# Start of the load order, the place of an arc tangent, and the engines of a power table in a fused state-space and feed-forward kernel

## The chip, the cores and the metric

One core of one Trainium2 chip runs the kernel. The metric is the device time of one execution in microseconds (us). TensorE (PE, with its weight load PEld), VectorE (DVE), ScalarE (ACT), GpSimd (POOL) and SyncE (SP) work side by side; DMAs are started from the queues of SP, ScalarE and GpSimd. Lines are named L12 and so on by their place in the kernel before.

## The reference, cut to what matters

```python
xn = layernorm(x)                         # x: 2048 rows of 576
# A: a long convolution of each of the 576 channels, by its response K
dt = exp(log_dt)
K[d, l] = Re( sum_n C[d, n] * exp(dt * A[d, n] * l) * dt * B[d, n] )      # n < 128, l < 2048
yA = causal_convolution(K, xn) + xn * Dskip
# B: a feed-forward layer
yB = silu(xn @ w1) @ w2                   # w1: 576 x 4608, w2: 4608 x 576
out = x + yA + yB
```

## The kernel before, in words

Rows of x are taken as 16 tiles of 128 (j = 0 to 15), each gathered by four loads of 32 partitions (`quarters`, L73), two tiles to a load (`load_x`, L161). `norm` (L174) takes the statistics on VectorE (L181, L182), the power -0.5 on GpSimd (L186), and the normalisation itself on VectorE for even tiles (L190) and on ScalarE for odd ones (L195). `put_xt` (L118) turns a tile over by TensorE (L122, L126) and splits it into a rounded part and the rest, xh and xl, ScalarE taking the first (L123, L127) and VectorE the second (L124, L128). Every product of the feed-forward layer is made of three matmuls of such parts.

The feed-forward layer (`ffn`, L229) goes over two halves of the rows, and in each over 9 chunks of 512 columns of w1, in blocks of four row tiles. `up` (L290) makes one 128 x 512 piece of the hidden layer in a PSUM tile ph (a ring of two), of which ScalarE makes gf and gh (L306, L307) and VectorE gl (L308); `down` (L310) multiplies by w2 into po (L328), which VectorE adds to acc (L333). The first block's `up` is done in two halves of 256 columns: tiles 0 and 1 first, tiles 2 and 3 after. Weights are loaded raw (w1r and w2r, L237 to L288) and split in the same way (L266, L268, L284, L286). In the second half a part of the products goes by a scheme with fewer multiplications (`wino_ffn`).

The other layer is a side line, a generator (`side`, L1024) that `weave` (L31) advances as the feed-forward layer comes on. It makes the tables of the response from the parameters (`natural`, L639: an arc tangent at L726 and a reciprocal root at L728, behind the last gh that was issued), tiles 8 to 15 in between; then the response (`kgen`, L756) in 36 steps of 16 channels, between some 150 and 650 us. A step makes angles, sines and magnitudes; every second step `powers` (L790) makes the powers 0 to 7 of four bases (lags 256, 64, 8 and 1) by multiplications on VectorE (L798 to L800) in the table pw, where only the powers 0 to 3 of lag 64 are used. TensorE sums over n (kp, L864) and transforms (z, L879); ScalarE puts the result into `stage` (L887), and after every fourth step two stores put it into DRAM (d1k, L892), each of 64 partitions with 64 runs of 32 numbers. In the same stretch `spread` (L138) transforms xn and stores it from GpSimd (d1u, L157), out of one buffer u1 for each of 32 steps. Afterwards `spectral` and `tail` finish the convolution.

What sets the order: each engine and each DMA queue runs its instructions in order, and that order isn't the one of the text. A planner arranges the instructions by a simulated timeline, by the order of the text as priority; `tc.high_priority()` lets an instruction go ahead, and `behind(ins)` (L135) keeps the instructions in its block behind `ins` on the same engine. At the start the side line runs tiles 0 to 3 wholly, then `ffn` asks for its first weights (the pair for t = 0 on GpSimd's queue, the rest on SP's) and splits them, then tiles 4 to 7 follow (L1077 to L1082). The loads of tiles 0 to 3 alternate between SP's and ScalarE's queues, and the stores of the first eight normalised tiles (dxn, L227) are SP's. From the beginning of `kgen` on, a second buffer w1x lets the raw first-layer weights be asked for a group ahead (`next_w1`, L253).

## Time and profile before

| | us |
|---|---|
| median of 3 runs | 1114.02 (1113.07 to 1114.62) |
| the profiled execution | 1115.58 |
| its span, first to last instruction | 1113.8 |
| TensorE busy in the span | 1090.6 |
| VectorE busy | 950.6 |
| ScalarE busy | 725.8 |
| GpSimd busy | 140.5 |

The granted TensorE clock was 1.00. Busy times overlap, so they don't add up to the span. In rows of the timeline the first number is the start and the second the duration, in us, of so many instructions (x4) in a row; what stands in square brackets is the idle time of the engine ahead of them and what ended it. In rows of groups, behind the bar, stand the busy time in us and the mean of one in ns, then the idle time ahead of them. Rows of waits give the sum in us, the number and the longest. Rows of one line give the smallest, middle and largest duration in ns and the first and last start in us. Rows of DMA issues end with the median time from issue to landing in us.

### The profile page before, as it was taken

The page shows a single profiled execution, that of the slowest core. Times are in us where ns is not written, and L with a number is a line of the kernel's source. Part 1 is how long each engine was busy: PE and PEld are TensorE (multiplying, and loading weights), DVE is VectorE, ACT ScalarE, POOL GpSimd, SP SyncE. Part 2 cuts the span into 40 slices and gives each one's busy share as a digit, 9 for nine tenths or more (in the row PEclk, how much of TensorE's full clock was granted, in tenths as well). Part 3 has the DMA queues.
Part 4 walks back from the last instruction along what each step waited for, and adds up shares of the span by engine and source line. Part 5 has one row for each costly group of instructions (what it writes and reads, how often), then busy time and mean ns, then how long its engine had stood idle before and what let it go on. Part 6 is the DMA issues. An engine that isn't in the chain of part 4 may idle for free.

```text
span 1113.8 us, 23080 instructions
## 1 busy us (share of the span) xinstructions
PE 1090.6 (98%) x9101; PEld 987.0 (89%) x9101; DVE 950.6 (85%) x1615; ACT 725.8 (65%) x1285; POOL 140.5 (13%) x244
## 2 busy tenths in 40 slices
PE   6999999999999999999999999999999999999998
PEld 5987989889988898898999888899899999999787
DVE  6699899999999999998999978989888988886333
ACT  4675455776767766667667646878687888775320
POOL 1022100000000000000330001121111211111220
PEclk9999999999999999999999999999999999999999
DMA  9445632436353536356964235465456555553985
GB/s 274 141 161 180 190 124 84 143 84 172 111 148 125 153 117 173 113 124 243 257 177 91 92 84 173 133 183 165 145 175 186 180 161 167 169 161 106 222 219 133
DMA packets 161869, 173.68 MB, mean 156 GB/s; under 512 B 88496, under 2 KB 127424, under 8 KB 161120
## 3 DMA queue, kind: packets, MB, share of 16 engines
q1 hardware_dynamic: 137200, 106.75, 34.4%
q0 software_dynamic: 23888, 63.67, 19.0%
q10 hardware_dynamic: 672, 1.77, 0.7%
q8 instruction: 72, 1.18, 0.4%
q14 instruction: 37, 0.30, 0.1%
HBM read 109.64 MB, written 62.60 MB: 155 GB/s over the span
## 4 chain that ended last, share of the span: by engine, by line
PE 83%; DVE 7%; DMA 5%; ACT 2%; issue 1%; POOL 0%; SPq 0%; DVEq 0%; ACTq 0%; POOLq 0%
PE po L328 35%; PE ph L298 19%; PE pb L453 6%; PE pc L453 3%; PE kp L864 3%; PE pu L996 2%; PE pk L996 2%; PE pb L996 2%; PE pa L453 2%; PE ph L299 2%; PE ph L300 2%; DMA w<-dw 1%; PE z L879 1%; DMA w1r<-in_B_w_dram 1%; PE pc L459 1%
## 5 line engine op out<-in xcount | busy, mean ns | idle before, releaser
L328 PE MATMUL po<-w,gh 128*128 128x288 f32 x2304 | 476.3, 297 | 5.1 <-DMA w<-dw 1.8
L328 PEld LDWEIGHTS po<-w,gh 128*128 128x128 f32 x2304 | 375.7, 188 | 21.9 <-issue 4.0
L328 PE MATMUL po<-w,gl 128*128 128x288 f32 x1152 | 334.7, 295 | 0.6 <-DVE gl L308 0.6
L328 PEld LDWEIGHTS po<-w,gl 128*128 128x128 f32 x1152 | 215.0, 188 | 2.6 <-DVE gl L308 0.9
L333 DVE TENSOR_TENSOR acc<-po,acc 128x288 f32<-128x288 f32 x296 | 130.1, 451 | 63.7 <-PE po L328 62.4
L298 PE MATMUL ph<-xh,w1h 128*128 128x512 f32 (+1 forms) x368 | 99.0, 387 | 0.9 <-ACT xh L123 0.6
L298 PE MATMUL ph<-xl,w1h 128*128 128x512 f32 (+1 forms) x368 | 98.4, 385 | 0.0
L298 PE MATMUL ph<-xh,w1l 128*128 128x512 f32 (+1 forms) x368 | 97.8, 382 | 0.0
L306 ACT ACTIVATE gf<-ph 128x512 f32<-128x512 f32 (+1 forms) x92 | 53.2, 579 | 59.2 <-PE ph L300 42.9
L298 PEld LDWEIGHTS ph<-xl,w1h 128*128 128x128 f32 x368 | 67.6, 191 | 12.9
L298 PEld LDWEIGHTS ph<-xh,w1l 128*128 128x128 f32 x368 | 66.4, 188 | 11.7
L298 PEld LDWEIGHTS ph<-xh,w1h 128*128 128x128 f32 x368 | 65.1, 191 | 11.2 <-ACT xh L123 0.9
L157 POOL DMA_DIRECT2D d1u<-u x32 | 17.5, 547 | 405.9 <-ACT u L156 404.6
L823 ACT ACTIVATE c<-th,magic 128x1040 f32<-128x1040 f32 x36 | 42.0, 1166 | 40.3 <-DVE C L844 28.3
L307 ACT CAST gh<-gf 128x512 fp32r<-128x512 f32 (+1 forms) x92 | 55.3, 602 | 14.6 <-PE po L328 13.7
L308 DVE TENSOR_TENSOR gl<-gf,gh 128x512 fp32r<-128x512 f32 (+1 forms) x92 | 60.7, 661 | 3.5 <-ACT gh L307 3.3
L901 POOL DMA_DIRECT2D m<-in_cm_dram x64 | 33.9, 531 | 234.0 <-PE pu L996 118.0
L825 ACT ACTIVATE c<-th 128x1040 f32<-128x1040 f32 x36 | 38.7, 1075 | 33.8 <-DVE th L824 33.6
L470 DVE TENSOR_TENSOR gl<-gf,gh 128x512 fp32r<-128x512 f32 x56 | 37.8, 688 | 19.1 <-ACT gh L469 18.5
L843 DVE TENSOR_TENSOR S<-th,C 128x1024 f32<-128x1024 f32 x36 | 43.9, 1221 | 11.7 <-ACT th L826 11.6
L824 DVE SCALAR_TENSOR_TENSOR th<-c,th 128x1040 f32<-128x1040 f32 x36 | 44.4, 1235 | 0.7 <-ACT c L823 0.6
L807 DVE TENSOR_TENSOR th<-vt,fT 128x1040 f32<-128x1040 f32 x36 | 44.4, 1235 | 0.0
(271 smaller groups left out, 2373.0 us busy)
## 6 DMA issues: line engine op xcount, KB each, us to landing
w1r<-in_B_w_dram SPq DMA_DIRECT2D x35, 512.0 KB, 4.2
dw<-w SPq DMA_DIRECT2D x28, 576.0 KB, 4.4
w<-dw POOLq DMA_DIRECT2D x28, 576.0 KB, 5.7
w2r<-in_B_w_dram SPq DMA_DIRECT2D x44, 288.0 KB, 5.0
d1u<-u POOLq DMA_DIRECT2D x32, 288.0 KB, 2.7
d1k<-stage SPq DMA_DIRECT2D x18, 512.0 KB, 7.2
ul<-d1u SPq DMA_DIRECT2D x32, 288.0 KB, 2.9
kl<-d1k SPq DMA_DIRECT2D x32, 288.0 KB, 3.4
```

The source lines that it names most:

```text
L298: nc.tensor.matmul(ph, w[:, kt, :], v[:, kt, a:e], start=n + kt == 0, stop=False)
L306: nc.scalar.activation(gf, ph, AF.Silu)
L307: pins["gh"] = nc.scalar.copy(gh, gf).ins
L308: pins["gl"] = nc.vector.tensor_sub(gl, gf, gh).ins
L328: pins["pe"] = nc.tensor.matmul(po[:, :HD], gs[g][:, js], ws[:, w, hs], start=n == 0 and j not in begun, stop=n == 3 * len(terms) - 1, ski ...
L333: nc.vector.tensor_add(acc[j][:, hs], po[:, :HD], acc[j][:, hs])
L453: pins["pe"] = nc.tensor.matmul(dst, a[:, kt], v[:, kt], start=start and n == 0, stop=stop and n == 5, skip_group_check=True).ins
L807: nc.vector.tensor_mul(split(th), row(vt[:, 0:65], 65), col(fT, i, 65))
L823: nc.scalar.activation(c65, th, AF.Identity, bias=magic)
L824: nc.vector.scalar_tensor_tensor(th, c65, MAGIC, th, op0=ALU.subtract, op1=ALU.subtract)
L843: nc.vector.tensor_mul(ov3, t[:, :, 0:64].rearrange("n d (x y) -> n d x y", y=32), mv3)
L996: nc.tensor.matmul(dst, st, mv[:, hs], start=n == 0, stop=n == 3 * len(terms) - 1)
```

## The change

Seven things change. Tiles 0 and 1 are loaded by eight loads of one tile instead of four of two, normalised one after the other, both on VectorE, and only then turned over, tile 0's xl behind tile 1's normalisation. The start goes in turns: loads of tiles 0 and 1; all six loads of the first w1 pieces, now all on SP's queue; tiles 0 and 1, then the loads of tiles 2 and 3, on SP's queue alone; loads of w2 and the w1 splits, the first of which is behind tile 0 on ScalarE and the others behind tile 1; tiles 2 and 3, behind tile 1; the w2 splits; tiles 4 to 7. The stores of normalised tiles 0 to 7 go to GpSimd's queue. The arc tangent is issued behind the latest odd tile's normalisation on ScalarE too. In the power table, ScalarE's Square makes powers 2 and 4, lag 64 comes last, and its powers 4 to 7 aren't made. The stores of the response go from SP's to GpSimd's queue. The buffer w1x is used from the third step of `kgen` on.

```diff
--- before.py
+++ after.py
@@ -115,13 +115,14 @@
         x4 = xtp.tile([P, 512], F32R, tag="x4", name=f"x4_{blk}")
         return xh, xl, x4
 
-    def put_xt(xh, xl, x4, src):
+    def put_xt(xh, xl, x4, src, low=None):
 
         pt = pss.tile([P, NKT, P], F32, tag="pss", name="pt")
         for kt in range(NKT):
             nc.tensor.transpose(pt[:, kt, :], src[:, kt * P:(kt + 1) * P], ident)
         nc.scalar.copy(xh, pt)
-        nc.vector.tensor_sub(xl, pt, xh)
+        with behind(low):
+            nc.vector.tensor_sub(xl, pt, xh)
         pt = pss.tile([P, 512], F32, tag="pss", name="pt4")
         nc.tensor.transpose(pt[:64, :P], src[:, NKT * P:D], ident)
         pins["xt_s"] = nc.scalar.copy(x4[:64, :], pt[:64, :P]).ins
@@ -161,8 +162,12 @@
     def load_x(j, pool, tag, engines):
 
         t = pool.tile([P, 2, D], F32, tag=tag, name=f"{tag}{j}")
-        for ps, v, eng in quarters(xv, engines):
-            eng.dma_start(t[ps], v[:, j:j + 2])
+        for i in range(j, j + 2, 1 if j == 0 else 2):
+            for ps, v, eng in quarters(xv, engines):
+                if j == 0:
+                    eng.dma_start(t[ps, i], v[:, i])
+                else:
+                    eng.dma_start(t[ps], v[:, j:j + 2])
         pairs[j] = t
         return t[:, 0, :], t[:, 1, :]
 
@@ -186,31 +191,35 @@
         pins["sd"] = nc.gpsimd.tensor_tensor(sd[:, :n], sd[:, :n], mhalf[:, :n], op=ALU.pow).ins
         xn = p0.tile([P, 2, D], F32, tag="xn", name="xn") if js[0] < 8 else pairs[js[0]]
         for i, j in enumerate(js):
-            if j % 2 == 0:
+            if j % 2 == 0 or n == 1:
                 pins["xn"] = nc.vector.tensor_scalar(xn[:, i, :], xs[i], mv[:, i, 0:1], sd[:, i:i + 1],
                                                  op0=ALU.subtract, op1=ALU.mult).ins
             else:
                 nc.vector.scalar_tensor_tensor(mb[:, i:i + 1], mv[:, i, 0:1], -1.0, sd[:, i:i + 1],
                                                op0=ALU.mult, op1=ALU.mult)
-                nc.scalar.activation(xn[:, i, :], xs[i], AF.Identity,
-                                     scale=sd[:, i:i + 1], bias=mb[:, i:i + 1])
+                pins["xo"] = nc.scalar.activation(xn[:, i, :], xs[i], AF.Identity,
+                                                  scale=sd[:, i:i + 1], bias=mb[:, i:i + 1]).ins
         return xn
 
     def phase0(p0, js):
         j0 = js[0]
         if j0 < 8:
-            xs = load_x(j0, accp, "acc", (nc.sync, nc.scalar) if j0 < 4 else (nc.sync,))
+            xs = load_x(j0, accp, "acc", (nc.sync, nc.scalar) if j0 == 0 else (nc.sync,))
             acc.update(zip(js, xs))
+            yield
         else:
             xs = load_x(j0, p0, "xj", (nc.sync,))
         if j0:
-            normed(p0, js, xs)
+            with behind(pins["xt1"] if j0 == 2 else None):
+                turned(p0, js, norm(p0, js, xs))
         else:
-            for j, xj in zip(js, xs):
-                normed(p0, (j,), (xj,))
-
-    def normed(p0, js, xs):
-        xn = norm(p0, js, xs)
+            xn = [norm(p0, (j,), (xj,)) for j, xj in zip(js, xs)]
+            last = pins["xn"]
+            for j in js:
+                turned(p0, (j,), xn[j], None if j else last)
+                pins[f"xt{j}s"] = pins["xt_s"]
+
+    def turned(p0, js, xn, low=None):
         for i, j in enumerate(js):
             b, jj = divmod(j, 4)
             if b < 2:
@@ -218,13 +227,12 @@
                     xts[b] = new_xt(b)
                 c = slice(jj * P, (jj + 1) * P)
                 xh, xl, x4 = xts[b]
-                put_xt(xh[:, :, c], xl[:, :, c], x4[:, c], xn[:, i, :])
+                put_xt(xh[:, :, c], xl[:, :, c], x4[:, c], xn[:, i, :], low)
             else:
                 xt = p0.tile([P, 9, P], F32R, tag="xt", name="xt", bufs=1)
                 put_xt(xt[:, 0:4, :], xt[:, 4:8, :], xt[:, 8, :], xn[:, i, :])
                 nc.gpsimd.dma_start(dxt[b - 2][:, :, jj * P:(jj + 1) * P], xt.bitcast(F32))
-        eng = nc.sync if js[0] < 8 else nc.gpsimd
-        eng.dma_start(dxn[:, js[0]:js[0] + len(js)], xn[:, :len(js)])
+        nc.gpsimd.dma_start(dxn[:, js[0]:js[0] + len(js)], xn[:, :len(js)])
 
     def ffn():
         w2v = w2.rearrange("(t p) d -> p t d", p=P)
@@ -240,7 +248,7 @@
             first = half == 0 and c == 0
             r1 = (pa if first and t else w1x if t and w1x else wp).tile([P, 5, 2 * P], F32, tag="w1r", name="w1r", bufs=1)
             fs = slice(f * P, (f + 2) * P)
-            eng = nc.gpsimd if first and t == 0 else nc.sync
+            eng = nc.sync
             eng.dma_start(r1[:, 0:4, :], w1[0:512, fs].rearrange("(k p) f -> p k f", p=P))
             eng.dma_start(r1[0:64, 4, :], w1[512:576, fs])
             pins["load"] = eng.dma_start(r1[64:128, 4, :], w1[512:576, fs]).ins
@@ -262,7 +270,7 @@
                 h1 = wp.tile([P, 5, P], F32R, tag="w1h", name="w1h", bufs=FT + 1)
                 l1 = wp.tile([P, 5, P], F32R, tag="w1l", name="w1l", bufs=FT + 1)
                 src = r1[:, :, i * P:(i + 1) * P]
-                with behind(pins.get("gh", pins["xt1s"] if t else None)):
+                with behind(pins.get("gh", pins["xt1s" if t + i else "xt0s"])):
                     nc.scalar.copy(h1, src)
                 with behind(pins["xt1"] if first else None):
                     pins["w1l"] = nc.vector.tensor_sub(l1, src, h1).ins
@@ -345,10 +353,12 @@
 
         for t in (0, 2):
             load_w1(0, 0, t)
+        yield 0
+        for t in range(FT):
+            load_w2(0, 0, t)
         for t in (0, 2):
             split_w1(0, 0, t)
-        for t in range(FT):
-            load_w2(0, 0, t)
+        yield 0
         for t in range(FT):
             split_w2(0, 0, t)
         yield 0
@@ -685,7 +695,7 @@
 
         ex = nat.tile([P, 4 * D], F32, tag="ex", name="ex")
         r = nat.tile([P, 4 * D], F32, tag="r", name="r")
-        for k, lag in enumerate((256.0, 64.0, 8.0, 1.0)):
+        for k, lag in enumerate((256.0, 8.0, 1.0, 64.0)):
             nc.scalar.activation(ex.rearrange("n (d k) -> n k d", k=4)[:, k, :], lrT, AF.Tanh, scale=0.5 * lag)
         yield
 
@@ -722,7 +732,7 @@
         v.tensor_scalar(t1, t1, 1.0, None, op0=ALU.add)
         yield
 
-        with behind(pins["gh"]):
+        with behind(pins["gh"]), behind(pins["xo"]):
             last = nc.scalar.activation(t0, t0, AF.Arctan).ins
         with behind(last):
             last = nc.scalar.activation(bi, t1, AF.Abs_reciprocal_sqrt).ins
@@ -793,13 +803,14 @@
                 nc.scalar.copy(pw[:, :, :, :, 1].rearrange("n q (g c) k -> n q g (c k)", g=2),
                                bases.pop(0).rearrange("n g (q c) k -> n q g (c k)", q=2))
                 load_bases(i + 2)
-                pv = pw.rearrange("n r d k e -> n (r d k) e")
-                R = 2 * W * 4
-                nc.vector.tensor_mul(pv[:, :, 2], pv[:, :, 1], pv[:, :, 1])
-                nc.vector.tensor_mul(pv[:, :, 3:5], pv[:, :, 1:3], pv[:, :, 2:3].broadcast_to([P, R, 2]))
-                nc.vector.tensor_mul(pv[:, :, 5:8], pv[:, :, 1:4], pv[:, :, 4:5].broadcast_to([P, R, 3]))
+                pv = pw.rearrange("n r d k e -> n (r d) k e")
+                nc.scalar.activation(pv[:, :, :, 2], pv[:, :, :, 1], AF.Square)
+                nc.scalar.activation(pv[:, :, 0:3, 4], pv[:, :, 0:3, 2], AF.Square)
+                nc.vector.tensor_mul(pv[:, :, :, 3], pv[:, :, :, 1], pv[:, :, :, 2])
+                nc.vector.tensor_mul(pv[:, :, 0:3, 5:8], pv[:, :, 0:3, 1:4],
+                                     pv[:, :, 0:3, 4:5].broadcast_to([P, 2 * W, 3, 3]))
                 for q in range(2):
-                    nc.vector.tensor_mul(split(al[:, q]), split(pw[:, q, :, 1, 0:4]), col(rhoT, i + q, 4))
+                    nc.vector.tensor_mul(split(al[:, q]), split(pw[:, q, :, 3, 0:4]), col(rhoT, i + q, 4))
                 return al
 
             def head(i):
@@ -831,8 +842,8 @@
                     ak.unsqueeze(2).broadcast_to([P, W, 8, 4]))
                 nc.vector.tensor_mul(
                     mag[:, :, 32:96].rearrange("n d (x y) -> n d x y", y=8),
-                    pk[:, :, 2, :].unsqueeze(3).broadcast_to([P, W, 8, 8]),
-                    pk[:, :, 3, :].unsqueeze(2).broadcast_to([P, W, 8, 8]))
+                    pk[:, :, 1, :].unsqueeze(3).broadcast_to([P, W, 8, 8]),
+                    pk[:, :, 2, :].unsqueeze(2).broadcast_to([P, W, 8, 8]))
                 if i + 1 < NCK:
                     nxt = head(i + 1)
                     if i % 2 == 1:
@@ -889,7 +900,7 @@
                     d0 = (i // NRUN) * NRUN * CH
                     kv = d1k.rearrange("(k n) (g d) -> g n k d", n=64, g=2)
                     for gp_ in range(2):
-                        nc.sync.dma_start(kv[gp_, :, :, d0:d0 + NRUN * CH], stage[gp_ * 64:(gp_ + 1) * 64])
+                        nc.gpsimd.dma_start(kv[gp_, :, :, d0:d0 + NRUN * CH], stage[gp_ * 64:(gp_ + 1) * 64])
                 yield (i + 1) / NCK
 
         nc.gpsimd.dma_start(d1k.rearrange("(k n) d -> n k d", n=P)[0],
@@ -1028,7 +1039,9 @@
         with tc.tile_pool(name="pa", bufs=4) as pa:
             for js in ((0, 1), (2, 3), (4, 5), (6, 7)):
                 with behind(pins["xt3"] if js[0] > 2 else None):
-                    phase0(pa, js)
+                    for _ in phase0(pa, js):
+                        if js[0] <= 2:
+                            yield 0
                 pins[f"xt{js[1]}"], pins[f"xt{js[1]}s"] = pins["xt_v"], pins["xt_s"]
                 if js[0] == 2:
                     yield 0
@@ -1046,14 +1059,16 @@
                     else:
                         j = next(tiles)
                         with behind(pins["gl"]):
-                            phase0(pb, (j, j + 1))
+                            for _ in phase0(pb, (j, j + 1)):
+                                pass
             with behind(pins["sd"]):
                 nc.gpsimd.dma_start(f1, cf1)
             nc.sync.dma_start(vt, cv)
-            with tc.tile_pool(name="up", bufs=1) as up, tc.tile_pool(name="w1x", bufs=1) as w1x:
+            with tc.tile_pool(name="up", bufs=1) as up, tc.tile_pool(name="w1x", bufs=1) as more:
                 sp = spread(up)
                 for n, at in enumerate(kgen()):
                     if n > 1:
+                        w1x = more
                         next(sp, None)
                     yield marks[0] + at * (marks[1] - marks[0])
                 for _ in sp:
@@ -1074,11 +1089,9 @@
         yp = ctx.enter_context(tc.tile_pool(name="yp", bufs=3))
         yield from tail()
 
-    sd = side()
-    next(sd)
-    fg = ffn()
-    next(fg)
-    next(sd)
+    sd, fg = side(), ffn()
+    for g in (sd, fg, sd, fg, sd, fg, sd):
+        next(g)
     weave(fg, 276, sd)
     for j in range(8, 14, 2):
         store(pairs[j], j, (nc.sync, nc.scalar))
```

## The prediction

> **What bounds the kernel now.** First the page's head, then the busy times by stretch.
>
> ```profile
> span 1113.8 us, 23080 instructions
> PE 1090.6 (98%) x9101; PEld 987.0 (89%) x9101; DVE 950.6 (85%) x1615; ACT 725.8 (65%) x1285; POOL 140.5 (13%) x244
> ```
>
> ```profile
> core 0: us, PE busy (x) PEld busy (x) DVE busy (x) ACT busy (x) POOL busy (x), PEclk, DMA share, GB/s
> 0.00:30.00 30.00, 19.38 (x128) 18.16 (x129) 21.07 (x61) 15.00 (x31) 6.22 (x13) 1.00 0.96 266
> 60.00:150.00 90.00, 86.99 (x531) 78.02 (x530) 82.69 (x149) 52.00 (x79) 15.18 (x17) 1.00 0.60 192
> 150.00:650.00 500.00, 498.89 (x5139) 449.94 (x5140) 476.93 (x704) 338.73 (x504) 37.34 (x72) 1.00 0.48 137
> ```
>
> TensorE has 1113.8 - 1090.6 = 23.2 us without work, and no instruction of the change takes a matmul away, so only idle time can be won: 10.6 us before 30, 3.0 us between 60 and 150, 1.1 us in the 500 us in which the response is made (150 to 650). The rest lies in parts that the change doesn't touch. So the Squares and the stores, both in the long stretch, can win at most 1.1 us however much VectorE they save (it is busy 476.93 of 500 there, yet TensorE hardly waits for it). What counts is the start and the stretch from 60 to 150.
>
> The start, in order of time:
>
> ```profile
> 0.74 1.78 SPq L165 DMA_DIRECT2D acc<-in_A_u_dram  x4
> ...
> 5.62 1.54 DVE L181 BATCH_NORM_STATS2 st<-acc 128x6 f32<-128x288 f32 x4 [4.69 <-DMA acc<-in_A_u_dram]
> 7.54 1.22 POOL L186 TENSOR_TENSOR sd<-sd,mhalf 128x1 f32<-128x1 f32 x2 [3.72 <-DVE sd L185]
> 8.15 0.58 DVE L190 TENSOR_SCALAR xn<-acc,mv,sd 128x576 f32<-128x576 f32 x1 [0.55 <-POOL sd L186]
> 8.79 1.11 PE L122 MATMUL pt<-ident,xn 128*128 128x128 f32 x4 [8.79 <-DVE xn L190]
> 8.99 0.87 ACT L195 ACTIVATE xn<-acc,mb,sd 128x576 f32<-128x576 f32 x1 [6.29 <-DVE mb L193]
> 9.39 1.54 DVE L181 BATCH_NORM_STATS2 st<-acc 128x6 f32<-128x288 f32 x4 [0.43 <-DMA acc<-in_A_u_dram]
> 10.76 1.35 ACT L266 CAST w1h<-w1r 128x640 fp32r<-128x640 f32 x2
> ...
> 12.02 0.58 ACT L123 CAST xh<-pt 128x512 fp32r<-128x512 f32 x1
> ...
> 12.65 2.08 PE L298 MATMUL ph<-xh,w1h 128*128 128x256 f32 x8 [0.58 <-ACT xh L123]
> 27.07 0.40 PE L328 MATMUL po<-w,gl 128*128 128x288 f32 x1 [0.63 <-DVE gl L308]
> ```
>
> Tiles 0 and 1 lie in the same four loads, so neither is begun before 5.62. The first projection matmul (12.65) waits for tile 1's xh, which ScalarE comes to last: ahead of it stand the normalisation of tile 1 (0.87) and two weight casts (1.35). At 27.07 TensorE has caught up with VectorE and waits for a gl.
>
> The chain of waits says what the loads wait for:
>
> ```profile
> 0.74 3.39 DMA acc<-in_A_u_dram
> 4.15 8.00 DMA w1r<-in_B_w_dram
> ...
> 17.26 5.05 DMA acc<-in_A_u_dram
> 22.34 1.54 DVE st L181 x4
> ```
>
> Each load here starts when an earlier one has landed (0.74 + 3.39 = 4.13, then 4.15; 17.26 + 5.05 = 22.31, then 22.34): four loads of SP and as many of ScalarE are out, and the ninth is held at the head of SP's queue until the first has landed. The order of the loads thus sets everything up to 22.
>
> Between 60 and 150, from the timeline, a row of VectorE, then ScalarE's, then TensorE's:
>
> ```profile
> 92.93 0.15 DVE L193 SCALAR_TENSOR_TENSOR mb<-mv,sd 128x1 f32<-128x1 f32 x1
> ```
>
> ```profile
> 96.23 1.28 ACT L726 ACT_TABLE_LOAD   x1
> ...
> 98.38 1.28 ACT L728 ACT_TABLE_LOAD   x1
> 99.68 0.84 ACT L728 ACTIVATE bi<-t 96x768 f32<-96x768 f32 x1
> 100.43 0.85 ACT L195 ACTIVATE xj<-xj,mb,sd 128x576 f32<-128x576 f32 x1
> ...
> 103.95 0.60 ACT L306 ACTIVATE gf<-ph 128x512 f32<-128x512 f32 x1
> ```
>
> ```profile
> 101.33 0.66 PE L122 MATMUL pt<-ident,xj 128*128 128x128 f32 x4 [1.73 <-ACT xj L195]
> ...
> 105.26 1.07 PE L298 MATMUL ph<-xh,w1h 128*128 128x512 f32 x4
> ```
>
> **The start, part by part.** *Loads.* Eight loads of 72 KB take the place of eight of 144 KB, and tile 0 is the first four. Before 5.62 four loads of 144 KB had to land; now half of that. These 288 KB at 246 GB/s (row below) are 1.2 us, so tile 0's statistics begin near 4.5.
>
> ```profile
> 2.00:6.00 4.00, 0.00 (x0) 0.00 (x0) 0.38 (x1) 0.69 (x2) 1.83 (x3) 1.00 0.99 246
> ```
>
> *First transposes.* One tile's statistics are half of 1.54 (0.77), its aggregate and sum some 0.35 together, the power 1.22 / 2 = 0.61, the normalisation 0.58: 2.3 us after 4.5, at 6.8 instead of 8.79. Tile 1's normalisation goes from ScalarE to VectorE (+0.58 there, -0.87 on ScalarE). *First projection.* From the start of the transposes there come these (1.11), then on ScalarE xh (0.58), the small copy (some 0.25), one weight cast (1.35 / 2 = 0.68) and tile 1's xh (0.58): 3.2 us, where it was 12.65 - 8.79 = 3.86. It begins near 10.0, 2.6 us earlier, if the weights are there: now all six weight loads are SP's and go out behind tiles 0 and 1 alone; 590 + 64 + 655 KB at 246 GB/s from about 2 us on are in at 7.4, and a receipt later at 8. *Tiles 2 and 3* come behind the second weight load too: 655 + 590 KB more at that rate end near 12.5, where their statistics began at 9.39. They are needed when the first half of the first block is through, near 18, and the way from statistics to xh takes about 5 us: just enough, and no cover is left over. *VectorE* is what gives part back: its work up to the wait at 27.07 begins 1.1 us earlier and grows by 0.58 - 0.15. So this term lies between 0.7 (VectorE busy throughout) and 2.6 + 0.63 = 3.2 (its statistics of tiles 4 to 7 move out of the way); I take 2.0, because the chain above shows that loads which now go out earlier held the statistics at 22.34 back.
>
> *The normalised tiles' stores* leave SP for POOL's queue: five issues of SP out of the way of loads, five on POOL of about 0.54 us (L157 below), which has 6.22 busy of 30. A later power behind such a store would wait for the tile's normalisation, at most its 0.87; I take nothing.
>
> **The arc tangent.** Tile 13's input was ready on VectorE's side by 93.08, but ScalarE did two table loads and two functions first, 4.2 us. Placed behind that normalisation, they let it run at 96.23, and the wait of 1.73 goes. What is late next: the third ph from there (105.26) needs the bank that the gf at 103.95 empties, ending at 104.55. All of ScalarE's work from 96.23 to there stays and is only reordered; TensorE would be there at 105.26 - 1.73 = 103.53, and 1.02 of the 1.73 would come back as a new wait unless the gf is also put ahead of the casts and the multiplication that follow. Between 0.7 and 1.7; I take 1.4, since gf is issued with high priority.
>
> **The powers.**
>
> ```profile
> L799 DVE TENSOR_TENSOR pw<-pw 128x256 f32<-128x256 f32 x18 | 11.3, 628 | 0.1
> L800 DVE TENSOR_TENSOR pw<-pw 128x384 f32<-128x384 f32 x18 | 9.9, 552 | 0.2
> L798 DVE TENSOR_TENSOR pw<-pw 128x128 f32<-128x128 f32 x18 | 7.7, 428 | 0.0
> L793 ACT COPY pw<-eb 128x128 f32<-128x128 f32 x18 | 8.0, 442 | 3.6 <-DVE C L832 3.4
> ```
>
> VectorE had 428 + 628 + 552 = 1608 ns a time, and keeps one multiplication of 128 (428) and one of 288 (under 552): some 0.65 less, 18 times, 11.7 us. ScalarE gets two Squares of 128 and 96 with the copy's stride, 0.44 each by L793: 0.88, 18 times, 15.9 us on an engine that is busy 338.73 of 500. VectorE's next multiplication now waits for ScalarE's queue, where a gf can stand waiting for TensorE. Of TensorE's waits in this stretch one is for ScalarE; beside it stands one from the group of weights before, near 139:
>
> ```profile
> PE po L328 <- ACT gh L307: 0.5, 1, 0.5
> ```
>
> ```profile
> PE ph L298 <- ACT w1h L266: 0.3, 1, 0.3
> ```
>
> The gain is at most the 1.1 without work; the loss at most 15.9, if every Square stood ahead of a gh that TensorE waits for. I take nothing. *The reserve for the first layer's weights* is taken into use some two steps of the response later, so one more group of weights is loaded as those before it, without an early request; such a group cost the wait of 0.3, so between 0 and 0.3, taken as nothing.
>
> **The stores of the response.**
>
> ```profile
> d1u<-u POOLq DMA_DIRECT2D x32, 288.0 KB, 2.7
> d1k<-stage SPq DMA_DIRECT2D x18, 512.0 KB, 7.2
> ```
>
> ```profile
> L157 POOL DMA_DIRECT2D d1u<-u x32: 539/539/592, 183.4 to 640.2; - x32
> L225 POOL DMA_DIRECT2D dxt<-xt x8: 955/968/1005, 72.3 to 130.6; - x8
> ```
>
> Each writes 64 x 64 runs of 32 numbers, 4096 pieces. POOL takes 539 ns for 128 pieces (L157) and 968 for 1152 (L225), 0.42 ns a piece, so 2.2 us by that slope, 4.4 a pair. Behind a pair stands a d1u store, whose single buffer ScalarE refills every (640.2 - 183.4) / 31 = 14.7 us: hidden while a pair takes less than some 11. SP is free of the pair; nothing of TensorE's waited for it. Nothing, then.
>
> [...]
>
> [...]
>
> **Sum.** 2.0 + 1.4 = 3.4 us. The profiled execution took 1115.58, its span 1113.8; the span becomes 1110.4, and the median of the runs, 1114.02, becomes 1110.6.
>
> **Rivals.** *Everything pays*: 3.2 + 1.7 + 1.1 = 6.0, 1108.0. For it: all the waits are in the rows. Against: VectorE's load at the start. *One of the two is given back*: tiles 2 and 3 come too late, or the gf holds TensorE, or the planner leaves the order as it was: 1.4 or 2.0 remain, 1112.0 to 1112.6. *The Squares hold up ScalarE* (slower): they stand in bursts with the sines, ahead of a gh. Each costs TensorE up to 0.88; from (3.4 + 2.2) / 0.88 = 6.4, so from 7 of the 18 on, the kernel is slower; with 9 it is 3.4 - 7.9 = +4.5, 1118.5. For it: the wait for gh above is of this sort. Against: it is one in 500 us. *POOL is held up by its 4096 pieces* (slower): if a store held POOL as long as one from SP takes to land, 7.2, a pair takes 14.4 and with the landing of d1u (2.7) is 14.4 + 2.7 - 14.7 = 2.4 too long, nine times: +21.6 - 3.4, 1132.
>
> **Chances.** A measurement of this kernel can tell 0.2%, 2.2 us, from no change. The forecast (1109.4 to 1111.8) 0.46, everything pays 0.18: faster 0.64. One given back: 0.18, within 0.2%. The Squares 0.12, POOL 0.06: slower 0.18. The range from 1107.5 to 1115.0 leaves out the end of the second case and the slow ones beyond.
>
> **What would show it.** First transposes near 6.8, first L298 near 10; no wait of TensorE for tile 13's xj, and L726 behind it; TensorE's idle time between 150 and 650 still near 1; the response's stores near 2.2 each on POOL. I am wrong if the idle time of the first 30 us stays at 10.6, if TensorE waits for gh or kp in the long stretch, or if d1u's copies wait for POOL.

## The result and the profile after

The changed kernel takes 1117.74 us (median of 20 runs), the kernel before 1113.94 (20 runs beside them): a ratio of 1.0025, 95% interval 1.0015 to 1.0036. The medians lie 3.8 us apart, the means, which the ratio compares, 2.9: it is **slower, by some 3 to 4 us**, where 1110.6, 3.4 us less than the 1114.02 known then, was predicted. The profiled executions don't show that difference: 1115.69 (span 1113.9) stands against 1115.58 (span 1113.8), because the one lies 2 us below the median of its kernel and the other 1.6 above. So the profiles serve to see where time is won and lost; what a part costs is taken from the medians below. Rows of a run have the line numbers of its own kernel: L157, L158, L882, L890 and L903 of the changed kernel are L156, L157, L871, L879 and L892 of the kernel before.

The page of the changed kernel:

```profile
span 1113.9 us, 23097 instructions
PE 1092.8 (98%) x9101; PEld 988.7 (89%) x9101; DVE 940.8 (84%) x1597; ACT 736.2 (66%) x1320; POOL 172.2 (15%) x264
```

VectorE has 9.8 us less to do, ScalarE 10.4 more, and GpSimd 31.7 more. Now by stretch, as before (columns: span, then busy time of PE, PEld, DVE, ACT, POOL, the granted clock, DMA share, GB/s):

```profile
0.00:30.00 30.00, 20.37 (x135) 18.31 (x136) 20.40 (x56) 14.23 (x32) 4.63 (x11) 1.00 0.93 265
60.00:150.00 90.00, 89.34 (x550) 80.84 (x549) 79.40 (x145) 52.30 (x81) 15.76 (x18) 1.00 0.59 188
150.00:650.00 500.00, 495.66 (x5052) 446.14 (x5050) 472.53 (x695) 351.85 (x540) 64.08 (x88) 0.99 0.47 138
```

TensorE's idle time fell from 10.6 to 9.6 in the first 30 us and from 3.0 to 0.7 between 60 and 150. In the long stretch it rose from 1.1 to 4.3, and the granted clock there is no longer 1.00.

**The start**, from the timeline:

```profile
7.03 1.11 PE L122 MATMUL pt<-ident,xn 128*128 128x128 f32 x4 [7.03 <-DVE xn L195]
7.13 0.15 DVE L190 TENSOR_SCALAR sd<-mv 128x1 f32<-128x1 f32 x1
7.29 0.60 POOL L235 DMA_DIRECT2D dxn<-xn  x1 [1.20 <-DVE sd L190]
7.91 0.59 POOL L191 TENSOR_TENSOR sd<-sd,mhalf 128x1 f32<-128x1 f32 x1
9.17 1.11 PE L122 MATMUL pt<-ident,xn 128*128 128x128 f32 x4 [0.81 <-DVE xn L195]
10.95 1.23 PE L306 MATMUL ph<-xh,w1h 128*128 128x256 f32 x4 [0.46 <-ACT xh L123]
14.34 1.54 DVE L186 BATCH_NORM_STATS2 st<-acc 128x6 f32<-128x288 f32 x4 [0.81 <-DMA acc<-in_A_u_dram]
21.96 0.30 PE L127 MATMUL pt<-ident,xn 128*64 128x128 f32 x1 [0.81 <-DVE xl L125]
```

The first transposes come at 7.03 (6.8 was said), but the first projection only at 10.95 (10.0 was said). Between them stands the store of tile 0: it is on GpSimd's queue at 7.29, and tile 1's power, whose sum is there at 7.28, begins behind it at 7.91. Tiles 2 and 3 are later than said: their statistics begin at 14.34 (12.5 was said), and TensorE waits 0.81 for their xl at 21.96.

**The arc tangent** went where it was put: tile 13's normalisation at 100.51, the first table load behind it, the transposes right after. No wait stands on the last row:

```profile
100.51 0.88 ACT L200 ACTIVATE xj<-xj,mb,sd 128x576 f32<-128x576 f32 x1
101.41 1.28 ACT L736 ACT_TABLE_LOAD   x1
...
102.62 0.60 PE L122 MATMUL pt<-ident,xj 128*128 128x128 f32 x4
```

**The long stretch.** ScalarE's waits by what ended them, then TensorE's (total, times, longest; kt is ScalarE's copy of kp, which the transform z reads); the first line has no counterpart before, where these copies waited for TensorE's pu alone:

```profile
ACT u L157 <- DMA d1u<-u: 12.4, 5, 5.6
```

```profile
PE z L890 <- ACT kt L882: 2.9, 2, 2.6
```

The place where it costs most, from the timeline:

```profile
325.49 3.29 POOL L903 DMA_DIRECT2D d1k<-stage  x2 [14.99 <-ACT u L157]
...
328.85 0.57 POOL L158 DMA_DIRECT2D d1u<-u  x1
...
341.76 0.70 ACT L157 COPY u<-pu 128x288 f32<-128x288 f32 x2 [5.58 <-DMA d1u<-u]
...
349.61 2.08 PE L890 MATMUL z<-f,kt 64*128 64x128 f32 x16 [2.58 <-ACT kt L882]
```

Read it downwards. GpSimd issues a pair of stores of the response, 3.29 us for both, and the store of u directly behind them, done by 329.42: GpSimd itself is free. But u lands only when ScalarE's next copy into u1 may begin, at 341.7, some 12.8 us after its issue, the longest landing of the 32 (2.9 in the middle). ScalarE stood 5.58 for it; kt, which comes behind that copy, a cast and four functions in ScalarE's order, was late; and TensorE waited 2.58 for kt. What follows is in the granted clock (last column but two):

```profile
340.00:349.00 9.00, 7.03 (x165) 6.54 (x163) 5.78 (x7) 5.65 (x8) 0.56 (x1) 1.00 0.25 77
349.00:356.00 7.00, 6.39 (x35) 6.17 (x36) 7.00 (x14) 4.46 (x10) 0.00 (x0) 0.52 0.04 9
356.00:360.00 4.00, 4.00 (x28) 3.76 (x28) 3.98 (x7) 4.00 (x8) 0.54 (x1) 1.00 0.02 8
```

From 348.96 TensorE ran at half its clock (0.50 in the mean up to 355.79) for 6.83 us, which is at most another 3.4 us of work; what of it was lost stands with e12 and e13 below. This is no accident of one execution: of the 20 runs of the changed kernel 18 have a mean clock of 0.998 or less, of the 104 runs of the kernel before that stand beside the experiments 18.

### The profile page after: what moved, and what is told of

The parts are those of the page before. It is cut to its first block, busy times and chain, and to the rows that moved or that the text cites. A ratio compares the mean times of both kernels' runs of the same rounds, so it can differ in the third digit from the quotient of the medians.

```text
span 1113.9 us, 23097 instructions
## 1 busy us (share of the span) xinstructions
PE 1092.8 (98%) x9101; PEld 988.7 (89%) x9101; DVE 940.8 (84%) x1597; ACT 736.2 (66%) x1320; POOL 172.2 (15%) x264
## 2 busy tenths in 40 slices
DMA packets 90989, 173.68 MB, mean 156 GB/s; under 512 B 14832, under 2 KB 54400, under 8 KB 90240
## 4 chain that ended last, share of the span: by engine, by line
PE 82%; DMA 6%; DVE 4%; issue 4%; ACT 2%; POOL 1%; SPq 0%; POOLq 0%; DVEq 0%; ACTq 0%
PE po L336 35%; PE ph L306 16%; PE pb L463 6%; PE pc L463 3%; PE kp L875 3%; PE pb L1007 2%; PE pk L1007 2%; PE pu L1007 2%; PE z L890 2%; PE pa L463 2%; PE ph L307 1%; PE ph L308 1%; DMA d1u<-u 1%; PE pc L469 1%; PE pu L155 1%
## 5 line engine op out<-in xcount | busy, mean ns | idle before, releaser
L315 ACT CAST gh<-gf 128x512 fp32r<-128x512 f32 (+1 forms) x92 | 55.4, 605 | 12.8 <-PE po L336 11.6
L158 POOL DMA_DIRECT2D d1u<-u x32 | 17.9, 558 | 274.7 <-ACT u L157 274.7
L903 POOL DMA_DIRECT2D d1k<-stage x18 | 29.6, 1647 | 133.1 <-ACT u L157 100.8
```

What stands on the lines that cost most here:

```text
L315: pins["gh"] = nc.scalar.copy(gh, gf).ins
```

## The experiments

Four letters for the parts: S the start (with the reserve for the weights), A the arc tangent, Q the Squares, P the response's stores on GpSimd's queue (POOL). Each row has the ratio to runs of the kernel before on the same chip. e1 to e4 share theirs, as do e5 to e8, e9 to e11 and e12 to e15; medians of different groups can be 1 us off against one another, since that kernel's own median lay between 1113.9 and 1115.2.

| kernel | parts | median, us | ratio, 95% interval |
|---|---|---|---|
| changed | S A Q P | 1117.74 | 1.0025 (1.0015 to 1.0036) |
| e1 | S A Q | 1114.69 | 1.0005 (0.9994 to 1.0015) |
| e2 | P | 1120.50 | 1.0052 (1.0036 to 1.0069) |
| e3 | S A P | 1118.32 | 1.0039 (1.0026 to 1.0051) |
| e4 | S A Q P, u stored by ScalarE | 1119.06 | 1.0045 (1.0032 to 1.0057) |
| e9 | S A Q P, u stored by SP | 1119.11 | 1.0052 (1.0032 to 1.0072) |
| e5 | S | 1124.53 | 1.0086 (1.0065 to 1.0107) |
| e6 | A | 1116.99 | 1.0025 (1.0008 to 1.0043) |
| e7 | Q | 1113.48 | 0.9984 (0.9971 to 0.9997) |
| e8 | S A | 1113.89 | 0.9992 (0.9980 to 1.0003) |
| e11 | A Q | 1117.02 | 1.0022 (1.0008 to 1.0037) |
| e12 | S A Q, one store of each pair on POOL | 1114.71 | 0.9995 (0.9979 to 1.0012) |
| e13 | S A Q, four of nine pairs on POOL | 1117.76 | 1.0017 (1.0001 to 1.0033) |
| e14 | S A Q, u stored by SP | 1117.70 | 1.0024 (1.0008 to 1.0041) |
| e15 | as e13, u stored by SP | 1116.63 | 1.0014 (0.9993 to 1.0034) |
| e10 | S A Q, tiles 0 and 1 stored by SP | 1112.76 | 0.9984 (0.9973 to 0.9995) |

### Which part costs: the stores (e1, e2, e3)

```diff
-                        nc.gpsimd.dma_start(kv[gp_, :, :, d0:d0 + NRUN * CH], ...)   # e1; e2 the other way round, on before
+                        nc.sync.dma_start(kv[gp_, :, :, d0:d0 + NRUN * CH], ...)
```

> The changed kernel with one part undone: the response's stores are SP's again, all else as changed. Theory 1 (each store of u to d1u stands in GpSimd's queue behind two stores of the response of 512 KB and lands late, ScalarE's next copy into the single buffer u1 waits for it, and TensorE waits for ScalarE): the copies' waits on d1u of up to 5.6 us go, landing of d1u falls from at most 12.8 to some 6 us, TensorE's idle time from 150 to 650 falls from 4.3 to about 1, no half clock near 350, and the time falls by 3.4 and a half clock's 3.4 at most: 1110 to 1114, that is 0.994 to 0.997 of the changed kernel. Theory 2 (the Squares hold ScalarE up, and the stores only add to it): it stays within 0.15% of the changed kernel, 1117, and the idle time stays near 4.

> The kernel before, with one part alone: the response's stores on GpSimd's queue, the powers still VectorE's. Theory 1 (d1u behind the response's stores in one queue): the copies into u1 wait for d1u here as well, up to some 5 us, TensorE's idle time from 150 to 650 grows from 1.1 to 4 or more, and the kernel is 3 to 7 us slower than before: 1117 to 1121. Theory 2 (the Squares): without them nothing is lost, within 0.15% of the kernel before, 1114.

e3 puts the three multiplications of VectorE back (the diff's lines on `pv`, `al`, the lags and `mag`, reversed).

> The changed kernel with the other part of the long stretch undone: the powers are three multiplications of VectorE again, the response's stores stay on GpSimd's queue. Theory 1 (queue): the waits of the copies into u1 for d1u stay, TensorE's idle time from 150 to 650 stays at 4 or more, the time stays near 1117 or rises by 1 to 3, since VectorE has 9.8 us more to do. Theory 2 (the Squares hold ScalarE up): TensorE's waits for z's kt go, and the time falls by about 3 to 1114.

The times of all three are as theory 1 has them, and theory 2 falls. Without the stores the changed kernel takes 3.05 us less (1117.74 to 1114.69, beside runs of the kernel before of 1113.94 and 1113.98); with nothing but the stores the kernel before takes 6.5 longer; without the Squares it stays slow. e2's profile has the same wait of ScalarE:

```profile
ACT u L156 <- DMA d1u<-u: 12.4, 5, 4.5
```

But the other half of its expectation, that TensorE's idle time in the long stretch grows to 4 or more, was missed: it is 1.4.

```profile
150.00:650.00 500.00, 498.57 (x5168) 449.57 (x5170) 475.40 (x702) 334.26 (x499) 63.91 (x88) 1.00 0.47 137
```

The profiled execution of e2 is 3.45 us below its median, and it doesn't show where the 6.5 us lie. In e3's, ScalarE waits 9.5 us for d1u, but TensorE's longest wait (3.13, at 338.94) is for a weight cast whose load came late. So these runs show that the stores cost time, and not by which way. e1 goes through the place shown above without it (the pair is SP's, and the copies wait for TensorE):

```profile
326.13 4.84 SPq L903 DMA_DIRECT2D d1k<-stage  x2
...
330.53 0.54 POOL L158 DMA_DIRECT2D d1u<-u  x1 [18.90 <-ACT u L157]
337.76 0.70 ACT L157 COPY u<-pu 128x288 f32<-128x288 f32 x2 [0.44 <-PE pu L156]
```

The Squares are innocent: e7, which has them alone, is the one part that is faster than the kernel before (see below).

### The queue, or the stores as such (e4, e9)

```diff
-                nc.gpsimd.dma_start(
+                nc.scalar.dma_start(                        # e4; nc.sync in e9
                     d1u.rearrange("(p m j) d -> m j p d", m=2, j=NJ)[m, j], u1)
```

> The changed kernel with the response's stores still on GpSimd's queue, but the 32 stores of u to d1u issued by ScalarE, on a queue of their own, right behind the copy that fills u1. Theory 1 (the queue's order, not the stores as such): d1u lands in 2 to 6 us again, the copies' waits for it go, and the time falls to 1111 to 1115; 32 issues on ScalarE may cost it some 0.1 us each, off the end. A rival to it, theory 3 (GpSimd's descriptors of 128 bytes slow all transfers down, whatever the queue): d1u lands late on ScalarE's queue too, and the time stays near 1117. Theory 2 (Squares): near 1117 as well, but with d1u landing early.

> The changed kernel with the response's stores still on GpSimd's queue, and the 32 stores of u to d1u on SP's queue (on ScalarE's queue their issues cost ScalarE 326 ns each, 10.4 us in all, which hid the answer). Theory 1 (d1u is late because it stands in one queue behind 1 MB of the response): d1u lands in 2 to 6 us, the copies' waits for it go, and the time falls to that of the changed kernel with the response's stores on SP, 1113 to 1115.5. Theory 3 (stores of 128-byte pieces made by GpSimd slow the kernel down whatever stands behind them): it stays at 1117 to 1119, with few waits of the copies on d1u. SP may now be held by the wait for u's copy with weight loads behind it: then TensorE's waits are for w1h or w.

Both seem to speak for theory 3: the copies' waits on d1u are gone but for one of 0.8 us in e4 and one of 3.8 in e9, and the time stays at 1119. But neither is a clean test. On ScalarE each issue takes 326 ns, 10.4 us for 32, on the engine whose delay is in question (operation, count, least, middle and longest ns, first and last start):

```profile
L158 ACTq DMA_DIRECT2D d1u<-u x32: 326/326/355, 191.4 to 635.5; - x32
```

And a change of a queue can make the planner lay the program out anew: in e9's trace 3138 of TensorE's 9101 matmuls stand at another place in the order than in the changed kernel's. With the order still open as a fourth theory, a test was wanted that moves stores and keeps the order.

### The same order, other queues (e12 to e15)

With half of the stores moved the planner leaves the order of e1: in e12 the lists of TensorE, VectorE and ScalarE are e1's line for line, in e13 but for a few lines of ScalarE. In e14's trace 135 of the 9101 matmuls stand at another place than in e1's, and in e15's 18 at another than in e14's.

```diff
-                        nc.gpsimd.dma_start(kv[...])
+                        (nc.sync, nc.gpsimd)[gp_].dma_start(kv[...])                              # e12
+                        (nc.gpsimd if i // NRUN < 4 else nc.sync).dma_start(kv[...])              # e13, e15
+                        nc.sync.dma_start(kv[...])                                                # e14; u on nc.sync in e14, e15
```

> The changed kernel with the first store of each pair of the response on SP's queue and the second on GpSimd's: half of the moved work, in the order of the kernel with all of them on SP (the same on TensorE, VectorE and ScalarE). Theory 1 (d1u late behind the stores): 512 KB instead of 1 MB stand ahead of d1u, which lands some 4 us earlier than in the changed kernel; a wait of 1 to 2 us of the copies at one or two places, at most 1 us on the time: 1114.5 to 1115.5. Theory 3 (each store made by GpSimd costs): half of 3, 1116. Theory 4 (the order of the instructions is the cost): as with all on SP, 1114.0 to 1114.7, whatever d1u does.

> The changed kernel with the first four of the nine pairs of the response on GpSimd's queue, both stores of a pair, and the last five on SP's: again the order of the kernel with all on SP but for ten lines of ScalarE. The waits at 282 and near 341 of the changed kernel lie in these four. Theory 1: they come back, 2 to 6 us of ScalarE's, TensorE waits for kt near 347 with the half clock behind it, and the time is 2 to 4 above that with all on SP: 1116.5 to 1118.5. Theory 3: 4 of 9, 1.5 to 2.5 above, 1116 to 1117. Theory 4: 1114 to 1114.7.

> The changed kernel with the response's stores and those of u to d1u all on SP's queue, the control for the next one: nothing of the response on GpSimd. If SP, held at u's copy, keeps weight loads back, it is slower than the 1114.7 with u on GpSimd's queue, by 1 to 4; if not, 1114 to 1115. All theories on the stores of the response expect the same here.

> The control (u's stores on SP) with the first four pairs of the response on GpSimd's queue, in the control's order; d1u can't stand behind them. Theory 1: as the control, within 1 us. Theory 3: 1.5 to 2.5 above the control. Theory 4: as the control.

e12 and e13 move nearly the same number of stores (nine and eight of 18) in the same order, and differ by 3.05 us. With 512 KB ahead of it (e12), u is in time at this place (one wait of 2.1 us for d1u is left elsewhere):

```profile
326.46 0.64 SPq L903 DMA_DIRECT2D d1k<-stage  x1
326.74 1.65 POOL L903 DMA_DIRECT2D d1k<-stage  x1 [14.75 <-ACT u L157]
...
330.42 0.56 POOL L158 DMA_DIRECT2D d1u<-u  x1 [2.04 <-ACT u L157]
338.09 0.70 ACT L157 COPY u<-pu 128x288 f32<-128x288 f32 x2 [0.44 <-PE pu L156]
```

With a whole pair, 1 MB, ahead (e13), the wait of the changed kernel comes back within 0.3 us of its size, the wait for kt with it, and the half clock (from 352.83, 3.41 us; 0.66 in the mean from 352 to 357):

```profile
327.25 3.28 POOL L903 DMA_DIRECT2D d1k<-stage  x2 [14.92 <-ACT u L157]
...
330.60 0.57 POOL L158 DMA_DIRECT2D d1u<-u  x1
...
343.78 0.70 ACT L157 COPY u<-pu 128x288 f32<-128x288 f32 x2 [5.84 <-DMA d1u<-u]
...
351.62 0.60 PE L890 MATMUL z<-f,kt 64*128 64x128 f32 x6 [2.84 <-ACT kt L882]
```

A mean clock of 0.998 or less stands in 11 of e13's 12 runs and in 2 of e12's 12.

TensorE's order is the same in e1, e12 and e13, and in the changed kernel up to 451 us, so that their matmuls can be compared one by one. Here is the first of z in e12, then in e1:

```profile
348.42 1.16 PE L890 MATMUL z<-f,kt 64*128 64x128 f32 x16
```

```profile
348.09 1.16 PE L890 MATMUL z<-f,kt 64*128 64x128 f32 x16
```

Just ahead of it e13 is 0.3 us behind e12, and the changed kernel 1.1 ahead of e1. At it they are 3.2 (351.62) and 1.5 (349.61) behind, at 360 3.8 and 3.3. So this one place costs e13 3.5 us and the changed kernel 4.5, in one execution of each: 2.9 and 2.6 by the wait for kt, and 0.6 and 1.8 behind it, while the clock was half.

Theory 4 falls with this pair, and so does theory 3: e12 has one store more on GpSimd's queue than e13 and is no slower than e1 (0.9995 and 1.0005 of the kernel before). e15 against e14 says less than was hoped. e15 has e13's stores with u on SP's queue and is not slower than e14 (1116.63 against 1117.70), but the runs of the two spread over 8 and 5 us, and e14 is no clean control. With nothing of the response on GpSimd it is slow by itself, 3.0 us above e12 (1117.70 against 1114.71), as its expectation allowed, and its trace has ScalarE wait 8.5 us for u again: on SP's queue u stands behind the same pairs and behind weight loads. The longest of these waits:

```profile
560.18 0.70 ACT L157 COPY u<-pu 128x288 f32<-128x288 f32 x2 [5.09 <-DMA d1u<-u]
```

How much of e9's time is of this kind was not tried, nor what the issues on ScalarE take of e4's. So theory 1 stands for the changed kernel and e13, while e2's loss is not traced to its place: **u's store is late because 1 MB of the response stands ahead of it in GpSimd's queue** (ScalarE waits 5.84 us for it in e13, and not at this place behind 512 KB in e12).

### The gains that didn't arrive (e5, e6, e7, e8, e11)

e5 is the changed kernel with P, Q and A undone, e8 the same with A kept, e6 the kernel before with this, e7 with the diff's lines of Q, e11 with both:

```diff
-        with behind(pins["gh"]):
+        with behind(pins["gh"]), behind(pins["xo"]):
             last = nc.scalar.activation(t0, t0, AF.Arctan).ins
```

> The kernel before, with the start's part alone (tiles 0 and 1 singly, the weights ahead of tiles 2 and 3, the normalised tiles' stores on GpSimd's queue, the reserve for the weights later): no Squares, response's stores SP's, arc tangent at its old place. Theory A (what TensorE gains at the start arrives at the end): the profiles show 1.0 us less idle time in the first 30 us, so 1113, 0.999 of before, and the wait of 1.7 for tile 13's xj near 100 is there again. Theory B (it is given back later, by the other order in which the pieces fall or by new waits): 1114 to 1115, not faster, though the first 30 us show 9.6 us idle and not 10.6.

> The kernel before, with the arc tangent placed behind tile 13's normalisation and nothing else. Theory A: the idle time from 60 to 150 falls from 3.0 by the 1.4 of the prediction or by the 2.3 seen in the changed kernel, and the time with it: 1111.7 to 1112.6, 0.998 to 0.9987 of before. Theory B: the wait at 100 goes but stalls of the same size come later, 1114.

> The kernel before, with the Squares on ScalarE alone; the response's stores stay SP's. Theory 1 (the stores are what costs): as the prediction had it, nothing, within 0.1% of before, 1113 to 1115. Theory 2 (the Squares cost something of their own beside the stores): TensorE's idle time from 150 to 650, 1.1 before, grows to 3 or 4 as it does in the changed kernel with the stores on SP, with waits near 390 to 410, and the time rises by 2 to 3, to 1116 or 1117.

> The changed kernel without the two parts of the long stretch: powers on VectorE and the response's stores on SP as before, start and arc tangent as changed. Theory A (gains add up): 1.0 + 2.3 = 3.3 less than before, 1110.7, 0.997 of before; the terms of the prediction would then be right but for the stores and the Squares. Theory B (given back): 1113 to 1115, and the profile shows where between 150 and the end the idle time grows.

> The kernel before with the Squares and the arc tangent's new place, the start and the stores as before. If the parts add up: 2.8 (arc tangent alone) minus 0.8 (Squares alone), 1116. If what the arc tangent alone costs comes from where a wait of VectorE falls among its other work near 130 to 140 and not from the arc tangent, it needn't come again with another order: then the gain of some 1.7 to 2.3 at 100 stands beside the Squares' 0.8, and the time is 1111 to 1112.5, faster than both kernels.

The parts don't add up. S alone costs 10.3 us, A alone 2.8, both together nothing that can be told from the kernel before (0.9980 to 1.0003).

One reason is that the wait which A was to win isn't there in every execution. In e2 the arc tangent is at its old place and TensorE's order up to 257 us that of the kernel before, and no wait for tile 13's xj stands in its trace. ScalarE wasn't held there by a weight load, as it was in the kernel before (1.42 us, until 95.02), had been 1.7 us ahead already, and came to that normalisation at 97.19 instead of 100.43:

```profile
97.19 0.85 ACT L195 ACTIVATE xj<-xj,mb,sd 128x576 f32<-128x576 f32 x1
```

By 100 e2's matmuls are 3.2 us ahead of the kernel before's, and 3.0 of it were won from 90 on. e7's trace has the wait again; how often it comes isn't known.

e6 shows how a gain turns into a loss. Its wait for tile 13's xj is gone; then, 30 us on:

```profile
129.65 0.96 POOL L225 DMA_DIRECT2D dxt<-xt  x1 [6.19 <-DVE xt L128]
130.26 0.82 DVE L333 TENSOR_TENSOR acc<-po,acc 128x288 f32<-128x288 f32 x2
134.00 0.06 DVE L775 MEMSET magic<- 128x1 f32 x1 [2.91 <-DMA dxt<-xt]
...
136.47 0.44 DVE L333 TENSOR_TENSOR acc<-po,acc 128x288 f32<-128x288 f32 x1
...
136.97 0.55 PE L328 MATMUL po<-w,gh 128*128 128x288 f32 x2 [1.07 <-DVE acc L333]
...
140.25 0.85 PE L328 MATMUL po<-w,gh 128*128 128x288 f32 x2 [1.02 <-DVE acc L333]
```

A small memset that opens the response's tables waits 2.91 us for the store of the last turned tile. In the kernel before three accumulations came ahead of it (the last at 134.92) and it didn't wait; here they stand behind it, in order on VectorE, and TensorE waits for them, 1.07 and 1.02 us, and 0.45 in between for a weight cast. Its matmuls, in the order of the kernel before but for 300 of 9101, are 2.2 us ahead of that kernel's at 120 and 2.9 behind at 150. Half clock lies over it from 138.66 for 6.83 us:

```profile
138.00:146.00 8.00, 6.88 (x24) 5.76 (x25) 7.94 (x15) 6.79 (x9) 0.00 (x0) 0.57 0.75 249
```

e11 has the same memset waiting 2.4 us and a half clock of the same length from 141.29 (0.96 in the mean from 60 to 150; another of 3.41 from 707.91, 0.98 from 650 to 710), and all 12 of its runs have a mean clock of 0.998 or less. I had expected the stall not to come again in another order; that was wrong. In e8 the memset doesn't wait. e5's loss is spread, as its long stretch and its waits between 100 and 560 show, 7.5 us idle and five waits for VectorE's accumulations:

```profile
150.00:650.00 500.00, 492.50 (x5035) 441.09 (x5034) 476.02 (x701) 334.46 (x501) 36.77 (x71) 1.00 0.48 139
```

```profile
PE po L336 <- DVE acc L341: 5.2, 5, 1.8
```

In its trace 4932 of the 9101 matmuls stand at another place than in e8's, though one `behind` is all that was changed in the text. The wait for tile 13's xj, which its expectation had, is not in it. What in that order makes S alone so slow stays open.

### A version that beats both (e10)

```diff
-        nc.gpsimd.dma_start(dxn[:, js[0]:js[0] + len(js)], xn[:, :len(js)])
+        (nc.sync if js[0] < 2 else nc.gpsimd).dma_start(dxn[:, js[0]:js[0] + len(js)], xn[:, :len(js)])
```

It has this beside e1's edit, and e1's order on TensorE and ScalarE.

> The changed kernel with the response's stores and the stores of normalised tiles 0 and 1 on SP's queue, so that at the start tile 1's power no longer stands behind tile 0's store on GpSimd. If that store is what cost the start its second microsecond: first projection matmul near 10.2 instead of 10.95, 20.9 to 21.3 busy in the first 30 us, and 0.5 us less than the 1114.7 of the kernel with only the response's stores on SP. If TensorE's order from there on decides, which is the same in both kernels: no difference that can be measured, 1114 to 1115.

```profile
7.16 1.92 SPq L235 DMA_DIRECT2D dxn<-xn  x2
7.52 0.56 POOL L191 TENSOR_TENSOR sd<-sd,mhalf 128x1 f32<-128x1 f32 x1 [1.31 <-DVE sd L190]
10.54 1.22 PE L306 MATMUL ph<-xh,w1h 128*128 128x256 f32 x4 [0.42 <-ACT xh L123]
```

Tile 1's power no longer waits, the first projection begins 0.41 earlier, and the kernel is faster than the one before: 0.9984 (0.9973 to 0.9995), 1.8 us. As the best of fifteen versions, timed in one group only, it may owe some of this to luck. By its profile TensorE does 0.7 us more in the first 30 us than in e1, which has 20.38 busy:

```profile
0.00:30.00 30.00, 21.07 (x138) 19.40 (x139) 21.23 (x58) 14.71 (x33) 3.42 (x9) 1.00 0.93 263
```

Matmul by matmul it is 0.7 us ahead of e1 at 60 and 1.9 at 180; where the second part comes from is not traced. e7 is as fast within its interval.

## Why the prediction was wrong

Two steps failed. Of the 7.1 us between 1110.6 and 1117.74, 3.05 are the stores; the other 4.1 are the gains that the sum was made of and that didn't arrive, since e1, without the stores, takes 1114.69 and can't be told from the kernel before.

**The step that turned the sign** is the last term, "the stores of the response", with its "hidden while a pair takes less than some 11" and its "Nothing, then". It counted how long GpSimd is held, and there it was even too careful: 1.65 us a store by the row below, where 2.2 was taken.

```profile
L903 POOL DMA_DIRECT2D d1k<-stage x18: 1636/1648/1675, 217.1 to 659.7; - x18
```

```profile
d1k<-stage POOLq DMA_DIRECT2D x18, 512.0 KB, 8.9
```

What counted was landing. The store behind shares the queue with the pair, each of which lands 8.9 us after its issue in the middle (13.3 at the most), so u lands up to 12.8 us after its own. e12 and e13 show it, with no wait for u at this place behind one store and 5.84 us behind two. And the cover was taken from a mean: 14.7 us between stores of u, where at this place the copies are ready 7.3 us after the store's issue (341.76 - 5.58 - 328.85). The term measured 3.05 us (changed kernel against e1, and e13 against e12) instead of 0.

The **fourth rival** named the queue and the sign, but let GpSimd be held for 14.4 us a pair and priced it at +21.6; it had a chance of 0.06. That a store holds GpSimd for 7.2 us is not seen: the longest took 1675 ns, beside a VectorE that is busy 94%.

**The step that took the gain away** is to add up idle time won at two places as if it were time won at the end.

**The start** (2.0 said): first transposes right; the first projection 0.95 later than said, of which 0.41 come from the store that "I take nothing" was written of, as e10 shows (it holds the power back by 0.63), and the rest isn't traced; idle time 1.0 less instead of 2.0. Its range of 0.7 to 3.2 held for the idle time, but not for the kernel's time, as e8 shows.

**The arc tangent** (1.4 said, at most 1.7): in the changed kernel the idle time from 60 to 150 fell by 2.3, more than its wait; as the only edit it costs 2.8. The sum assumed that what is won at 100 stays won, which e6 refutes, and that the wait of 1.73 in the one profile is there in each execution, which e2 refutes. The second rival, in which one of the two is given back, came nearest for S and A: e8 gives back nearly both.

**The powers** (0 said): right within what can be told. e7 is 0.16% faster (0.03 to 0.29), so nothing like the loss of the third rival; e3 against the changed kernel shows no loss either.

Of the signs that the prediction named, "TensorE's idle time between 150 and 650 still near 1" failed (4.3). The way there was beside those named: TensorE waited for kt, not "for gh or kp", and the copies for the landing of d1u, not "for POOL".

## What to carry to other kernels

When a transfer moves to another queue, list what stands behind it there and add up landings, not issue times; and compare them with the shortest distance to the next use of that buffer, not the mean. A wait seen in one profile needn't be in the next execution: look for it in a second trace before it is priced. Near a full TensorE a stall had two prices here, its length (2.9 and 2.6 us) and what the half clock behind it cost (0.6 and 1.8). Where a planner orders the instructions, the gain of one edit holds for one order only: test parts in pairs that keep the order, and check that they do.

## What was not expected of the hardware

TensorE's clock falls to half (0.50 from 348.96 to 355.79 in the changed kernel), for 3.41 or 6.83 us: after one wait of 2.58 (changed kernel), 2.84 (e13) or, in e5, 1.82, with the half clock from 110.28 (0.57 and 0.58 in the mean of the two stretches of 2 us from 110 on), and after 1.07 and 0.45 within 2 us (e6); not after the single 1.73 at 101.33 in the kernel before, where it stays 1.00.

```profile
108.89 0.54 PE L336 MATMUL po<-w,gh 128*128 128x288 f32 x2 [1.82 <-DVE acc L341]
```

In these four cases some 1.5 to 2.8 us of idle time went ahead of the fall. In the changed kernel's trace the changes of the clock, at 348.96, 355.79 and 1113.54, lie 2 and 222 times 3.413 us apart (764.58 / 224 from the first to the last). Steps of this length, an estimate from these three changes, can be counted back from a fall, and where in a step a wait lies doesn't explain it: the 1.73 that did nothing lies within one step (99.11 to 102.53, counted from the fall at 1112.87 at the end of the kernel before), and so do the 1.82 (106.87 to 110.28) and the 1.07 and 0.45 (135.25 to 138.66). What decides stays open.

The 128-byte pieces of the response go from GpSimd's queue in larger packets: the changed kernel has 90989 packets instead of 161869 for the same 173.68 MB, and 14832 of under 512 B instead of 88496, 73664 fewer where the 18 stores have 73728 pieces. It buys nothing; a store lands in 8.9 us there and in 7.2 from SP, in the middle.
